# Attention's projection matmuls dealt 28 : 56 : 16 over a head pair's three steps

## The chip, the cores and the metric

The kernel runs on one core of a Trainium2 chip. The metric is the device time of one execution in microseconds, taken as the median of several runs. A core has five engines that work side by side and wait for each other through semaphores: TensorE (PE in the profile, with its weight loads as PEld), VectorE (DVE), ScalarE (ACT), GpSimd (POOL) and SyncE (SP), which here issues the DMAs.

## The reference

Two layers alternate, twice over, on a sequence of 2048 rows of width 640: an attention with a memory, and a gated mixer. Cut to what is computed:

```python
def attention(x, wq, wk, wv, wo, beta):          # 32 heads of 20, 4 segments of 512 rows
    for s in range(4):
        logits = q[s] @ k[s].T * scale + mask     # the mask adds -1e9 above the diagonal
        a_dot = softmax(logits) @ v[s]
        a_mem = (phi(q[s]) @ M) / (phi(q[s]) @ z + 1e-6)
        o[s] = g * a_mem + (1 - g) * a_dot        # g = sigmoid(beta), one per head
        M = M + phi(k[s]).T @ v[s];  z = z + sum(phi(k[s]))
    return o @ wo                                 # phi(t) = t + 1 where t > 0, else exp(t)

def mixer(x, w_in, w_sp, b_sp, w_out):
    z = gelu(x @ w_in);  z1, z2 = halves of z;  z2 = layernorm(z2)
    return (z1 * (w_sp @ z2 + b_sp)) @ w_out

x = x + attention(layernorm(x));  x = x + mixer(layernorm(x))   # and both once more
```

As its inputs say, q, k and v come from x through wq, wk and wv.

## The kernel before, in words

Each matrix is held as a pair of 16-bit parts, high and low, and a product is three matmuls: high by high, high by low, low by high. There are three stages per layer pair. `phase1a` (line 1082) is attention, `phase1b` (line 235) the last attention rows' output projection and the mixer's input projection, `phase2` (line 329) the mixer's spatial product and output projection. Attention alone is touched by the change; it runs twice.

Attention is written by hand as one order of work, in `Attention.run` (line 943). 128 rows of a segment and 128 rows of its keys meet in blocks; the blocks of one **head pair** (two heads, one segment) are dealt out over three **steps**. There are 64 head pairs, so 192 steps, and a few ahead and behind. At step t the loop at the end of `run` writes, in this order:

- `scores(n, c)` (line 829), c being t modulo 3. It makes two sets of score blocks in PSUM, each with a single buffer: `mp`, for the maxima of the pair two further on, which VectorE reduces to `mx` (line 871), and `es`, for the exponentials of this pair, which ScalarE writes to `P` (line 864). The rows of keys and queries are multiplied on line 855 and the mask is added by matmuls on line 827. In the first step the first block is 512 columns wide and there are 512 in all; in the second step the blocks are 384 and 128 wide, again 512; in the third, 256 only. The two heads of a pair go side by side. `mp` and `es` of a step can be written only when the reduction and the exponential of the step before have read them.
- what was posted for this step (`post`, line 548, puts a function on the list of a later step): evictions of the projections, key updates of the memory and others.
- `pvs` (line 896), the probability-times-value matmuls (line 908), for one head in the third step and for the other in the first. The second step has none. In the first step there is also `maxes` (line 885), which turns the maxima and stores them beside the queries by a DMA.
- `cast` (line 873), behind each `pvs`: ScalarE makes the 16-bit high part `PH` of a head's probabilities (line 881), GpSimd the low part `PL` (line 882). `combine` (line 912), VectorE's and GpSimd's work on a finished pair, comes in the second step, ahead of the scores.
- `until(t + 1)` (line 1043): all background streams that are due before the next step. There are four: the loads and layer norms (`fills`), weight preparation (`background`), the memory reads (`reads`, matmuls on lines 751 and 755), and **the projections** (`dense`, line 1003).

The projections are the q and k of a unit of heads (`unit`, line 678, matmuls on line 689, 512 columns wide), v of 128 rows (`value`, line 621, line 632, 320 wide) and the output projection of finished rows (`project`, line 650, line 665, 320 wide). All are groups of 15 matmuls into one of two PSUM buffers named `dn`. A group's eviction is posted one step after its end; for keys that feed the memory a second part (`keys`, line 720) is posted one step after that, and the buffer is read until its last operation on line 723. The stores of q and k (lines 798 and 799), the transposing DMA of the key features (line 725) and the loads of the pairs (`fetch`, line 803) are DMAs that SyncE issues in order.

When a projection matmul is due is a matter of a written table, not of measured times:

```python
PACE = (-LEAD, 2400), (0, 700), (53, 1150), (128, 1250), (END + G, 0)
```

It says from which step on how many nominal nanoseconds of projections go into a step. `step(w)` (line 964) turns the work done so far into a step with a fraction. `timed` (line 971) wraps each job: the job yields a nominal cost after each matmul (216 for q and k) or after three (408 for the narrow ones), and `timed` yields the time at which it wants to go on. So before the change the projections are spread evenly over the steps of a stretch of the table.

PE's instructions are issued in the order in which they are written (`manual_schedule` for PE, line 1085). The other engines' orders are a planner's, from the same program.

Of the kernel before, what the change touches and what calls it, by code (L numbers as in the profile page):

```python
# [454 lines left out]
KCH = ((0,), (1, 3), (2,))  # L455
QCH = ((3,), (2, 0), (1,))
BIG = 60000.0


def attn_consts(g, cp, beta):  # L460
# [6 lines left out]
    with tc.tile_pool(name="tmp", bufs=1) as tp, tc.tile_pool(name="acp", bufs=1, space=PSUM) as pp:  # L467
        f = tp.tile([128, 192], F32, name="fmask")
        for t, n, b, sg, op in ((g.big, 192, -64, 1, ALU.not_equal), (g.mask["q"], 128, 0, -1, ALU.is_ge), (g.mask["k"], 128, -64, 1, ALU.is_ge)):
            nc.vector.memset(f, 0.0)  # L470
            for h in range(2):
                v = f[64 * h:64 * h + 64, :n]
                nc.gpsimd.affine_select(v, v, [[sg, n]], op, BIG if op is ALU.not_equal else -BIG, base=b, channel_multiplier=-sg)
            nc.vector.tensor_copy(t, f[:, :n])
# [49 lines left out]
class Attention:  # L524
# [418 lines left out]
    def run(self, nseg=NSEG):  # L943
# [20 lines left out]
        def step(w):  # L964

            for (t, p), (e, _) in zip(PACE, PACE[1:]):
                if w <= p * (e - t):
                    return t + w / p
                w -= p * (e - t)

        def timed(it, done, work):
            end = done + work
            yield step(done)
            for w in it:
                done += w
                yield step(min(done, end))

        ev, jobs, acc = [], [], 0
        for c in order:
            w = V if c[0] in "vp" else U  # L980
            beg = step(acc)
            if c[0] in "vp":
                i = int(c[1:])
                s = i // 4
            if c[0] == "v":
                ev.append((beg - 11, 0, i))
                it = self.value(i)
                assert s < 2 or beg > G * (s - 1) + self.LV + 3, (i, beg)
            elif c[0] == "p":
                ev.append((beg - 3.5, 1, i))  # L990
                it = self.project(i)
                assert beg - 3.5 > G * (s + 1) + self.LV + 5, (i, beg)
            else:
                s, m = int(c[0]), int(c[1])
                it = self.unit(s, m)
                i = NU * s + m - 4
                for r in range(i, i + 1 + (i % NU < NU - 1)):
                    assert r < NU or beg > G * (r // NU) + 9 * (r % NU) - 3 + (3 if r % NU == 4 else 0), (s, m, r, beg)
                assert step(acc + w) < G * s + 9 * m - LEAD - 3, (s, m, step(acc + w))
            jobs.append(timed(it, acc, w))  # L1000
            acc += w
# [52 lines left out]
        for t in range(-LEAD, END):  # L1054
            self.now = t
            f, c = divmod(t + self.LF, 3)
            if c == 0 and 0 <= f + self.LM < N:
                self.fetch(f + self.LM)
            p, r = divmod(t - self.LV - 2, 3)
            if r == 0 and 0 <= p < N:  # L1060
                self.combine(p, *pairs[p])
            n, c = divmod(t, 3)
# [3 lines left out]
            for h in range(2):  # L1066
                p, r = divmod(t - self.LV - h, 3)
# [82 lines left out]
```

## Time and profile before

| what | value |
|---|---|
| median of 3 runs | 2474.31 us |
| lowest and highest | 2472.66, 2476.86 us |
| span of the profiled execution, first to last instruction | 2466.8 us |
| instructions | 50722 |
| mean granted TensorE clock | 0.974 of full speed |

The profiled execution's own time is known by its span alone: 2466.8 us, 7.5 us under the median of the runs, which holds also what lies before the first and after the last instruction. Attention lies at some 100 to 655 us of the span and at some 1300 to 1840 us.

In the profile's rows a group of instructions has its line, engine, operation, output and inputs by the program's names, shapes and count; behind the first bar the busy time and the mean length of one in ns, and behind the second the time for which the engine stood idle just before, with what ended it. In rows in order of time the first number is the start, the second the length, both in us from the span's start; brackets hold the idle time ahead. The durations of matmuls overlap, since they are pipelined; the distance from start to start is what one costs.

### The profile page before, as it was taken

What the parts mean: (1) busy time and instruction counts of PE and PEld (TensorE: products, weight loads), DVE (VectorE), ACT (ScalarE), POOL (GpSimd) and SP (SyncE); (2) the same over time, 40 slices, a digit from 0 to 9 for tenths busy, and PEclk for the clock granted to TensorE, in tenths of its full rate; (3) what the DMA queues carried; (4) which work ended last, traced back from release to release, by engine and by line L of the source; (5) the groups of instructions that cost most, each with busy time, mean ns of one, the idle gap of its engine ahead of it and who ended that gap; (6) DMA issues with size and microseconds to landing.
All of it is one profiled execution on the core that took longest, in us unless ns stands there. A gap on an engine that the chain in (4) does not pass through costs nothing.

```text
span 2466.8 us, 50722 instructions
## 1 busy us (share of the span) xinstructions
PE 2224.2 (90%) x20682; PEld 1317.4 (53%) x20682; DVE 1431.5 (58%) x2766; ACT 1137.3 (46%) x1388; POOL 937.1 (38%) x728
## 2 busy tenths in 40 slices
PE   3688888999899989999997888889997997999998
PEld 2355455666545545555554545565664554555554
DVE  8667877677754545544326777777764453453441
ACT  3278767777632222212124977777772222121110
POOL 3168777888610100000012988788872110000000
PEclk9899899999999999999999999999998998999999
DMA  6724644334553487767444352443446345766762
GB/s 198 207 56 101 172 107 113 100 108 123 140 162 94 114 221 193 189 155 173 101 137 124 74 123 69 112 113 86 126 128 145 94 114 151 167 166 155 173 128 58
DMA packets 502505, 325.00 MB, mean 132 GB/s; under 512 B 408512, under 2 KB 443456, under 8 KB 497152
## 3 DMA queue, kind: packets, MB, share of 16 engines
q1 hardware_dynamic: 502272, 321.76, 50.8%
q8 instruction: 162, 2.65, 0.5%
q14 instruction: 71, 0.58, 0.1%
HBM read 148.25 MB, written 85.34 MB: 95 GB/s over the span
## 4 chain that ended last, share of the span: by engine, by line
PE 56%; DVE 10%; ACT 10%; DMA 9%; issue 5%; SPq 3%; POOL 3%; ACTq 0%; DVEq 0%; POOLq 0%
PE gp L380 16%; PE zp L295 13%; PE cyp L409 6%; ACT PH L881 3%; ACT P L864 3%; PE vps L632 3%; PE pv L908 3%; DVE mx L871 3%; DMA wr<-in_B_w_sp_dram 2%; PE kps L689 2%; PE mp L855 2%; PE qps L689 2%; PE yps L665 2%; PE es L855 2%; POOL PL L882 2%
## 5 line engine op out<-in xcount | busy, mean ns | idle before, releaser
L882 POOL TENSOR_TENSOR PL<-P,PH 128x1280 f16<-128x1280 f32 x248 | 649.6, 2619 | 177.0 <-ACT PH L881 156.4
L380 PE MATMUL gp<-zh,wt 128*128 128x432 f16 x2048 | 466.6, 348 | 23.8 <-DMA wt<-wn 23.8
L871 DVE TENSOR_REDUCE mx<-mp 128x2 f32<-128x1024 f32 (+3 forms) x512 | 409.4, 816 | 130.2 <-PE mp L827 127.4
L380 PEld LDWEIGHTS <-wt 128*128 128x128 f16 x3072 | 301.8, 98 | 286.4 <-DMA wt<-wn 25.5
L864 ACT ACTIVATE P<-es,sc 128x1024 f32<-128x1024 f32 (+1 forms) x384 | 371.3, 967 | 161.6 <-PE es L827 160.0
L881 ACT CAST PH<-P 128x1280 f16<-128x1280 f32 x256 | 320.5, 1253 | 19.2 <-PE pv L908 12.8
L295 PEld LDWEIGHTS <-th 128*128 128x128 f16 x1920 | 188.6, 98 | 178.6 <-issue 10.4
L380 PE MATMUL gp<-zl,wt 128*128 128x432 f16 x1024 | 272.8, 348 | 0.0
L395 POOL MEMSET un<- 128x64 f16 x32 | 4.8, 151 | 672.5 <-DMA ut<-un 610.2
L205 POOL TENSOR_TENSOR lnrs<-lnve,mhalf 128x1 f32<-128x1 f32 x96 | 58.5, 617 | 467.7 <-DVE lnve L204 442.9
L855 PEld LDWEIGHTS <-qk 60*128 60x128 f16 (+1 forms) x2048 | 91.4, 93 | 261.3 <-issue 155.6
L383 ACT ACTIVATE u<-gp,bsp,un 128x864 f32<-128x864 f32 x32 | 34.2, 1070 | 363.3 <-PE gp L380 363.3
L357 DVE TENSOR_REDUCE am<-wr 128x1 f32<-128x2048 f32 x32 | 73.2, 2286 | 218.6 <-DMA wr<-in_B_w_sp_dram 218.6
L855 PE MATMUL mp<-qk 60*128 60x512 f16 (+3 forms) x1024 | 138.3, 307 | 55.9 <-DVE mx L871 55.0
L632 PE MATMUL vps<-wvh,xt 128*128 128x320 f16 x640 | 157.5, 310 | 27.2 <-DMA xt<-xnhl 14.5
L409 PE MATMUL cyp<-wuh,ut 128*128 128x320 f16 (+1 forms) x896 | 166.8, 303 | 11.9 <-DMA ut<-un 11.9
L855 PE MATMUL es<-qk 64*128 64x512 f16 (+3 forms) x1024 | 134.3, 298 | 47.3 <-ACT P L864 34.7
L409 PEld LDWEIGHTS <-ut 128*128 128x128 f16 (+1 forms) x1344 | 132.8, 99 | 69.9 <-DMA ut<-un 13.5
L827 PEld LDWEIGHTS <-big 64*128 64x128 f16 x3072 | 141.0, 95 | 50.5 <-issue 3.2
L908 PE MATMUL pv<-vs,PL 128*128 128x41 f16 x2560 | 163.0, 181 | 4.9 <-DVE PL L882 2.6
L908 PE MATMUL pv<-vs,PH 128*128 128x41 f16 x2560 | 166.3, 182 | 1.2 <-DVE ab L924 1.2
L295 PE MATMUL zp<-wi1h,th 128*128 128x432 f16 x640 | 150.2, 349 | 8.8 <-DMA th<-xnhl 8.8
(182 smaller groups left out, 4063.7 us busy)
## 6 DMA issues: line engine op xcount, KB each, us to landing
wr<-in_B_w_sp_dram SPq DMA_DIRECT2D x32, 1024.0 KB
qk<-st SPq DMA_DIRECT2D x256, 120.0 KB
x<-x SPq DMA_DIRECT2D x56, 320.0 KB
z<-z SPq DMA_DIRECT2D x32, 432.0 KB
cz<-z SPq DMA_DIRECT2D x32, 432.0 KB
xt<-in_A_x_dram SPq DMA_DIRECT2D x32, 320.0 KB
st<-qhl SPq DMA_DIRECT2D x40, 256.0 KB
st<-khl SPq DMA_DIRECT2D x40, 256.0 KB
```

Of the source, the lines that this page charges most:

```text
L295: nc.tensor.matmul(zp[:, n, :FHH], a[:, k, :], b[:, k, c:c + FHH], start=(k == 0 and j == 0), stop=(k == KD - 1 and j == 2))
L380: nc.tensor.matmul(gp[:, n, :FHH], wt[:, k // 8, a, k % 8, :], b[:, k, n * FHH:(n + 1) * FHH], start=(k == 0 and j == 0), stop=(k == NT - ...
L409: nc.tensor.matmul(yp[:, n, :320], a[:kn[k], k, :], b[:kn[k], k, n * 320:(n + 1) * 320], start=(k == 0 and j == 0), stop=(k == KO - 1 and ...
L632: nc.tensor.matmul(ps, a[:, k, c], b[:, k, n * 320:(n + 1) * 320], start=(i == 0), stop=(i == 14))
L689: nc.tensor.matmul(ps, a[:, k, c], b[:, k, :], start=(i == 0), stop=(i == 14))
L827: nc.tensor.matmul(out, g.big[r, 64 - 64 * s:192 - 64 * s], mk, start=False, stop=s == 1, skip_group_check=True)
L855: nc.tensor.matmul(out[:, h, o:o + w], a[r, ac], b[r, bc], start=o == 0, stop=False, skip_group_check=True)
L864: nc.scalar.activation(P[:, :, 512 * c:512 * c + ew], es[:, :, :ew], AF.Exp, scale=g.esc)
L871: nc.vector.tensor_reduce(self.mx[m][:, :, i], mp[:, :, o:o + w], AX.X, ALU.max)
L881: nc.scalar.copy(PH, P[:, h])
L882: (nc.gpsimd if h == 0 or n < self.N - self.TAIL else nc.vector).tensor_tensor(PL, P[:, h], PH, ALU.subtract)
L908: nc.tensor.matmul(pv[:, i, h, :], x[:, c:c + 128], v[:, j, h0 + h, :], start=(j == 0 and x is PH), stop=(j == i and x is PL), skip_group_ ...
```

## The change

A new constant gives three shares, and `share` maps a time within a head pair's three steps: the first 28 per cent of the pair's projection work goes behind the scores of its first step, the next 56 per cent behind the second, the last 16 behind the third. The amount per pair is the table's, as before. What is yielded inside a job goes through it; a job's first yield does not.

```diff
+DENSE = 0.28, 0.56, 0.16
...
+        def share(t):
+
+            p, r = divmod(t, 3)
+            done = 0
+            for c, f in enumerate(DENSE):
+                if r < 3 * (done + f) or c == 2:
+                    return 3 * p + c + min((r / 3 - done) / f, 0.999)
+                done += f
+
         def timed(it, done, work):
             end = done + work
             yield step(done)
             for w in it:
                 done += w
-                yield step(min(done, end))
+                yield share(step(min(done, end)))
```

## The prediction

> **What bounds the kernel now.** I read the page first, then the busy times by stretch, the groups with their forms kept apart, and the rows in order of time.
>
> ```profile
> span 2466.8 us, 50722 instructions
> ## 1 busy us (share of the span) xinstructions
> PE 2224.2 (90%) x20682; PEld 1317.4 (53%) x20682; DVE 1431.5 (58%) x2766; ACT 1137.3 (46%) x1388; POOL 937.1 (38%) x728
> ...
> PE 56%; DVE 10%; ACT 10%; DMA 9%; issue 5%; SPq 3%; POOL 3%; ACTq 0%; DVEq 0%; POOLq 0%
> ```
>
> Over the whole span PE is nearest to full, but only 56 per cent of the chain that ended last is PE; DVE and ACT hold 10 each. The change touches only the two attention stages, so I look at those, in three stretches that match the three paces of the projections: steps 12 to 59, 60 to 113, and 114 to 185.
>
> ```profile
> core 0: us, PE busy (x) PEld busy (x) DVE busy (x) ACT busy (x) POOL busy (x), PEclk, DMA share, GB/s
> 161.00:290.00 129.00, 108.17 (x1537) 63.58 (x1536) 101.74 (x196) 106.92 (x137) 105.03 (x64) 0.95 0.45 118
> 290.00:463.00 173.00, 150.68 (x1976) 94.36 (x1975) 130.93 (x252) 126.85 (x167) 131.01 (x93) 0.95 0.49 123
> 463.00:655.00 192.00, 183.97 (x2601) 119.44 (x2599) 139.78 (x276) 144.34 (x175) 156.43 (x106) 1.00 0.41 113
> ...
> 178.26:231.33 53.07, 47.74 (x737) 27.03 (x738) 41.92 (x81) 49.27 (x63) 48.01 (x28) 1.00 0.37 93
> ```
>
> In the first three rows the columns after the length are busy times. The third stretch is PE's: 184 of 192 us. In the second PE has 22 us of idle time, and no other engine is near full. The last row is an undisturbed part of the first stretch, 53.07 us long: ACT is busy for 49.27, POOL 48.01, PE 47.74. There ACT is the floor, and at most 53.07 - 49.27 = 3.8 us (7 per cent) can be had however PE's work is ordered.
>
> Where does PE wait? A step's chunk width tells it apart: 512 columns open the first step of a pair, 384 the second, 256 the third. So the idle time ahead of a form is the wait at the end of the step before.
>
> ```profile
> L855 PE MATMUL mp<-qk 60*128 60x512 f16 x256 | 51.3, 397 | 0.4 <-DVE mx L871 0.4
> L855 PE MATMUL es<-qk 64*128 64x512 f16 x256 | 49.4, 382 | 11.4 <-DMA qk<-mr 10.2 <-ACT P L864 0.9 <-ACT PH L881 0.3
> L855 PE MATMUL mp<-qk 60*128 60x384 f16 x256 | 43.4, 335 | 10.7 <-DVE mx L871 10.7
> L855 PE MATMUL es<-qk 64*128 64x384 f16 x256 | 41.9, 322 | 6.9 <-ACT P L864 6.3
> L855 PE MATMUL mp<-qk 60*128 60x256 f16 x256 | 36.3, 280 | 44.7 <-DVE mx L871 43.9
> L855 PE MATMUL es<-qk 64*128 64x256 f16 x256 | 35.7, 271 | 29.0 <-ACT P L864 27.5
> ```
>
> The idle time stands after the second bar. Ahead of the third step PE waits 44.7 + 29.0 = 73.7 us; ahead of the second 10.7 + 6.9 = 17.6; ahead of the first 0.4 and, for a DMA, 11.4. The wait sits behind the second step, the one step in which no probability-times-value matmuls run. One instance, in order of time:
>
> ```profile
> 201.75 0.39 PE L855 MATMUL mp<-qk 60*128 60x384 f16 x4
> 202.37 0.33 PE L827 MATMUL es<-maskk,big 64*128 64x128 f16 x4
> 202.85 0.59 PE L689 MATMUL qps<-xt,wqh 128*128 128x512 f16 x2
> 204.46 0.28 PE L855 MATMUL mp<-qk 60*128 60x256 f16 x2 [1.01 <-DVE mx L871]
> 205.78 0.38 PE L689 MATMUL qps<-xt,wql 128*128 128x512 f16 x1
> 206.00 0.59 PE L689 MATMUL qps<-xt,wqh 128*128 128x512 f16 x2
> 206.74 0.39 PE L855 MATMUL mp<-qk 60*128 60x512 f16 x2
> ...
> 202.71 0.50 DVE L924 TENSOR_TENSOR ab<-pv,rs 128x328 f32<-128x328 f32 x1
> 203.12 1.28 DVE L871 TENSOR_REDUCE mx<-mp 128x2 f32<-128x768 f32 x2
> 205.17 0.67 DVE L871 TENSOR_REDUCE mx<-mp 128x2 f32<-128x512 f32 x1
> ```
>
> The second step's scores and its three projections end by 203.44; VectorE reads the one score buffer until 204.40, after its combine work; the third step's scores start at 204.46. Behind the third step the maxima are ready at 205.84 and PE arrives at 206.74: a cushion of 0.90 us.
>
> **The change part by part.** It removes and adds no instruction; every matmul, load, eviction and DMA stays. Only the step behind which a projection matmul stands moves, inside its pair. Evaluating the code's own pace table gives the matmuls per step (first, second, third): first stretch 3.8, 3.4, 4.1 become 3.2, 6.0, 2.1; second 6.2, 6.2, 6.8 become 5.1, 10.9, 3.2; third 7.1, 7.5, 7.2 become 5.7, 12.5, 3.5. The granularity is fine enough for that: q and k matmuls move singly, the others in threes. From the rows above a q matmul takes 206.00 - 205.78 = 0.22 us of PE; one of the narrower kind takes 519.48 - 519.34 = 0.14:
>
> ```profile
> 519.34 0.30 PE L665 MATMUL yps<-woh,o 128*128 128x320 f16 x1
> 519.48 0.30 PE L665 MATMUL yps<-wol,o 128*128 128x320 f16 x1
> ```
>
> The first stretch is nearly all q and k, the second half and half, the third two thirds narrow. So the second step gains some 0.56, 0.85 and 0.8 us, the third loses 0.43, 0.65 and 0.6, the first 0.13, 0.19 and 0.22.
>
> *Waits ahead of the third step.* They fall by at most what the second step gains. The shares of the 73.7 us by stretch, first attention:
>
> ```profile
> L855 PE MATMUL mp<-qk 60*128 60x256 f16 x32 | 4.6, 287 | 9.2 <-DVE mx L871 9.2
> L855 PE MATMUL es<-qk 64*128 64x256 f16 x32 | 4.6, 276 | 4.6 <-ACT P L864 4.1
> ...
> L855 PE MATMUL mp<-qk 60*128 60x256 f16 x36 | 5.1, 280 | 7.7 <-DVE mx L871 7.7
> L855 PE MATMUL es<-qk 64*128 64x256 f16 x36 | 5.0, 271 | 6.2 <-ACT P L864 6.0
> ...
> L855 PE MATMUL mp<-qk 60*128 60x256 f16 x48 | 6.8, 279 | 4.8 <-DVE mx L871 4.5
> L855 PE MATMUL es<-qk 64*128 64x256 f16 x48 | 6.6, 269 | 2.6 <-ACT P L864 2.6
> ```
>
> That is 13.8, 13.9 and 7.4 us. Cutting each single wait at the gained time leaves some 7, 9.5 and 4.5 as coverable (a few waits are over 1.5 us and only partly covered); I take the second attention as like the first. What is realized of it I choose by the stretch's other engines. First stretch: ACT's 7 per cent room, so a third, 2 x 2.4 = 5 us. Second: idle PE, ACT and DVE at 73 to 76 per cent, so 60 per cent, 2 x 5.7 = 11. Third: PE-bound, a wait removed is time gained, 80 per cent, 2 x 3.6 = 7. Together 23 us; bounds 0 and 2 x 21 = 42. The steep start of each attention (steps before 12, no exponentials at first) I take as nothing, bounds 3 either way.
>
> *New waits ahead of the first and second steps.* The third step's cushion of 0.90 us covers 0.43 to 0.65; where it is smaller a little shows. The first step has less: PE already waits 17.6 us ahead of the second. If every one of the 128 pairs lost its first step's time anew, that is 128 x 0.2 = 26; at least nothing. Most pairs have no wait there, so I take 5 for both places.
>
> *The evictions behind the projections.* The accumulators have two buffers, and a group's eviction is written one step after its end (for keys a second part two steps after). A denser second step shortens the time until the buffer is wanted again. Such waits exist:
>
> ```profile
> PE kps L689 <- DVE phl L723: 25.6, 6, 8.3
> PE vps L632 <- DVE vs L638: 9.2, 4, 3.5
> ```
>
> By the code, groups reused under one step after their eviction is written rise from 5 to 8 in an attention. Three more in each of two attentions at 0.7 us are 4 us (25.6 / 6 and 9.2 / 4 are longer, but stand mostly at the start of an attention, where the paces crowd); bounds 0, and the 3.5 us of the longest value wait for all 16, 56.
>
> *DMAs and queues.* Each eviction takes its stores and its key transpose with it, on SP, earlier or later by under a step; they are read several steps on. The waits for a DMA (10.2 us ahead of the first step's scores) belong to the max rows, which keep their place, a whole pair ahead of use. I take nothing; a pair that gets shorter by 0.4 us takes as much cover from them, so up to 5 us. POOL gets no instruction moved, and its subtraction already ends late only where the cast before it does.
>
> Sum: -23 + 5 + 4 = -14 us. On the profiled span that is 2466.8 - 14 = 2452.8; the runs' median, 2474.3, lies 7.5 above the span, and I keep that distance: **2460 us**.
>
> The Trainium skill, Perfetto Trace Analysis, section Optimization Strategy, says that the same gap repeating on the engine that should be saturated can mean too little PSUM for the next tile. The trace agrees so far: the repeated wait is for the single score buffer, and no buffer is added here. By that rule alone the bubble would move instead of going, and the sum would be 0; it is the second rival.
>
> **The rivals.** *Evictions become the bound (slower).* Place: projection accumulators in the second and third stretch, where 11 to 12 projection matmuls, most of a group of 15, now run in one step. It decides once the key eviction's last VectorE operation ends after the third step's scores and its three matmuls. If the 16 close groups each stall PE by 2 us, between the 0.7 above and the 3.5, that is 32 in place of 4: -23 + 5 + 32 = +14, so 2488. Against it: PE waits for evictions little today outside the start. For it: DVE is 75 per cent busy and its queue is in order.
>
> *The bubble only moves (no change).* ACT's casts and exponentials hold 49.27 of 53.07 us in the clean part; if the second and third stretches follow ACT and DVE in the same way, the 23 shrinks to the 9 that new waits cost: 2474. For it: 27.5 us of the waits ahead of the third step end with ACT's exponential. Against it: ACT has 46 us of room in the second stretch's 173.
>
> *All is recovered (faster still).* 2 x 21 = 42 less 9 gives -33: 2441. It needs ACT to run full in the first stretch, which the 3.8 us there nearly forbid.
>
> That the change does not deal as it says I hold for excluded: PE's order is the written one.
>
> **How the numbers follow.** Forecast (2450 to 2468) 0.47, full recovery 0.13, no change 0.16, slower 0.24. A measurement of this kernel tells 0.2 per cent, 5 us, from no change. Faster takes the first two, 0.60; same 0.16; slower 0.24. The range reaches from full recovery, 2441, to the eviction rival, 2488, and leaves out about 0.07 below and 0.12 above. The forecast's own range is 2450 to 2468.
>
> **What would show it.** Right: idle time ahead of the 256-column forms falls from 73.7 to about 40 us, that ahead of the 384-column forms rises from 17.6 to some 20 to 25, and the third stretch's PE share rises. Wrong by evictions: waits of kps, qps, vps or yps for DVE grow by tens of us. Wrong by a moving bubble: the 384- and 512-column forms take over what the 256-column forms lose, with ACT's busy share unchanged. Wrong altogether would be a gain outside the two attention stages.

## The result and the profile after

The changed kernel takes 2444.64 us (median of 4 runs, 2440.32 to 2447.60) against 2473.48 (median of 4 runs of the kernel before beside them): a ratio of 0.9889, 95 per cent interval 0.9868 to 0.9910. That is 28.8 us off, about twice the 14 forecast. The spans of the two profiled executions differ by 28.2 us.

The page of the changed kernel, its span, its busy times and the engines' shares of the chain that ended last:

```profile
span 2438.6 us, 50718 instructions
## 1 busy us (share of the span) xinstructions
PE 2218.2 (91%) x20682; PEld 1319.0 (54%) x20682; DVE 1434.3 (59%) x2766; ACT 1133.7 (46%) x1388; POOL 936.1 (38%) x728
...
PE 60%; DVE 11%; DMA 11%; ACT 7%; issue 5%; POOL 3%; SPq 3%; ACTq 0%; DVEq 0%; POOLq 0%
```

PE's share of the chain rises from 56 to 60 per cent, ScalarE's falls from 10 to 7. The groups of the changed kernel with their forms apart show where PE now waits; idle time stands behind the second bar, and the lines shown carry a number one higher than before:

```profile
L856 PE MATMUL mp<-qk 60*128 60x512 f16 x256 | 50.8, 392 | 6.4 <-DVE mx L872 4.4 <-DVE lnve L204 0.8 <-DMA st<-khl 0.8
L856 PE MATMUL es<-qk 64*128 64x512 f16 x256 | 50.0, 384 | 15.1 <-DMA qk<-mr 12.3 <-ACT P L865 1.7 <-ACT PH L882 1.2
L856 PE MATMUL mp<-qk 60*128 60x384 f16 x256 | 43.3, 334 | 7.9 <-DVE mx L872 7.6
L856 PE MATMUL es<-qk 64*128 64x384 f16 x256 | 42.4, 325 | 9.6 <-ACT P L865 9.5
L856 PE MATMUL mp<-qk 60*128 60x256 f16 x256 | 36.3, 280 | 16.8 <-DVE mx L872 16.6
L856 PE MATMUL es<-qk 64*128 64x256 f16 x256 | 35.5, 271 | 16.8 <-ACT P L865 15.7
L890 PE MATMUL mtp<-ident,mx 128*8 128x128 f32 x128 | 34.9, 273 | 9.1 <-DVE gm L765 8.4 <-DVE mst L788 0.5
```

Ahead of the third step (256 columns) the wait falls from 73.7 to 16.8 + 16.8 = 33.6 us. Ahead of the second (384) it stays: 17.6 before, 17.5 now. Ahead of the first (512) it rises from 11.8 to 21.5. The last row is new as a wait: the transpose of the maxima, behind the first step's scores, had PE idle for 1.2 us ahead of it before and has 9.1 now. So 40.1 us went and 9.7 + 7.9 = 17.6 came.

One pair's second and third step of the changed kernel, in order of time (start, length; idle ahead in brackets). It is the pair that the prediction shows:

```profile
198.78 0.40 PE L856 MATMUL mp<-qk 60*128 60x384 f16 x4
199.00 0.34 PE L828 MATMUL mp<-maskq,big 64*128 64x256 f16 x4
199.19 0.40 PE L856 MATMUL es<-qk 64*128 64x384 f16 x4
199.40 0.34 PE L828 MATMUL es<-maskk,big 64*128 64x128 f16 x4
199.68 0.39 PE L690 MATMUL qps<-xt,wql 128*128 128x512 f16 x1
199.91 0.59 PE L690 MATMUL qps<-xt,wqh 128*128 128x512 f16 x2
200.34 0.38 PE L690 MATMUL qps<-xt,wql 128*128 128x512 f16 x1
200.55 0.38 PE L690 MATMUL qps<-xt,wqh 128*128 128x512 f16 x1
201.56 0.28 PE L856 MATMUL mp<-qk 60*128 60x256 f16 x2 [0.62 <-DVE mx L872]
```

Behind the second step's scores stand five q matmuls instead of three, and the third step's scores wait 0.62 us instead of 1.01. That is the change as meant: 0.4 us of work in a gap of one microsecond.

By stretch, from the changed kernel's busy times (length, PE, PEld, DVE, ACT, POOL with instruction counts; granted clock, DMA share, GB/s), and below them the same steps in the kernel before:

```profile
158.30:287.30 129.00, 107.35 (x1540) 62.89 (x1540) 104.07 (x197) 106.91 (x138) 104.58 (x64) 0.96 0.45 118
287.30:454.80 167.50, 146.76 (x1973) 94.03 (x1973) 132.78 (x251) 126.96 (x165) 131.02 (x93) 0.97 0.48 124
454.80:642.00 187.20, 182.91 (x2599) 119.63 (x2598) 137.98 (x277) 142.69 (x175) 155.90 (x106) 1.00 0.44 120
```

```profile
161.30:291.20 129.90, 109.07 (x1542) 63.95 (x1543) 102.94 (x198) 107.82 (x138) 104.73 (x64) 0.95 0.45 119
291.20:463.30 172.10, 149.78 (x1972) 94.02 (x1971) 129.73 (x250) 125.95 (x165) 131.01 (x93) 0.95 0.49 123
463.30:652.00 188.70, 181.31 (x2560) 117.72 (x2561) 136.78 (x273) 142.60 (x172) 154.77 (x105) 1.00 0.40 111
```

The first stretch hardly moves. The second loses 4.6 us. In the third PE goes from 181.31 of 188.70 us to 182.91 of 187.20, 96 to 98 per cent (this window takes in a little more work after the change). Measured from score start to score start, with the idle times of each stretch's groups added up, the two attentions together give (us, before to after; the last column is the difference):

| steps | wait ahead of the third step | of the second | at the first, with the transpose and the value matmuls | length |
|---|---|---|---|---|
| up to 11 | 4.5 to 1.4 | 4.7 to 5.2 | 0.0 to 0.0 | -4.1 |
| 12 to 59 | 27.3 to 15.1 | 4.6 to 8.9 | 2.6 to 11.1 | -4.4 |
| 60 to 113 | 27.5 to 14.6 | 8.4 to 3.1 | 3.8 to 12.4 | -13.6 |
| 114 to 179 | 9.0 to 0.0 | 0.0 to 0.0 | 1.9 to 3.1 | -8.3 |

The lengths sum to -30.4; the rest of the kernel gave back 2.3. The table holds the answer: everywhere the gap behind the second step about halves or goes. In the first stretch 12.2 us go and 12.8 come back at the other two steps; that it is shorter all the same goes with 2.3 us of waits for a key group's eviction, gone after the change, and with a PE that is busy for less time. In the second 8.6 come back at the first step, but 5.3 more go at the second; in the third almost nothing comes back.

### The profile page after: what moved, and what is told of

Its sections match the earlier page's. It is cut to its first block, busy times and chain, and to the rows that moved or that the text cites. A ratio compares the mean times of both kernels' runs of the same rounds, so it can differ in the third digit from the quotient of the medians.

```text
span 2438.6 us, 50718 instructions
## 1 busy us (share of the span) xinstructions
PE 2218.2 (91%) x20682; PEld 1319.0 (54%) x20682; DVE 1434.3 (59%) x2766; ACT 1133.7 (46%) x1388; POOL 936.1 (38%) x728
## 4 chain that ended last, share of the span: by engine, by line
PE 60%; DVE 11%; DMA 11%; ACT 7%; issue 5%; POOL 3%; SPq 3%; ACTq 0%; DVEq 0%; POOLq 0%
PE gp L380 16%; PE zp L295 14%; PE cyp L409 6%; PE pv L909 3%; PE yps L666 3%; PE kps L690 3%; DMA wr<-in_B_w_sp_dram 3%; PE vps L633 3%; PE mp L856 3%; PE qps L690 3%; ACT PH L882 2%; ACT P L865 2%; PE es L856 2%; POOL PL L883 2%; DVE mx L872 2%
## 5 line engine op out<-in xcount | busy, mean ns | idle before, releaser
L295 PEld LDWEIGHTS <-th 128*128 128x128 f16 x1920 | 188.9, 99 | 177.8 <-issue 11.7
L383 ACT ACTIVATE u<-gp,bsp,un 128x864 f32<-128x864 f32 x32 | 34.2, 1068 | 355.5 <-PE gp L380 355.5
L633 PE MATMUL vps<-wvh,xt 128*128 128x320 f16 x640 | 156.3, 310 | 22.5 <-DMA xt<-xnhl 13.8
L409 PEld LDWEIGHTS <-ut 128*128 128x128 f16 (+1 forms) x1344 | 132.6, 99 | 73.7 <-DMA ut<-un 17.4
L367 ACT ACTIVATE wn<-wr,ivw 128x1024 f16<-128x1024 f32 x64 | 71.9, 1144 | 194.6 <-DVE ivw L362 111.1
```

What stands on the lines that cost most here:

```text
L295: nc.tensor.matmul(zp[:, n, :FHH], a[:, k, :], b[:, k, c:c + FHH], start=(k == 0 and j == 0), stop=(k == KD - 1 and j == 2))
L409: nc.tensor.matmul(yp[:, n, :320], a[:kn[k], k, :], b[:kn[k], k, n * 320:(n + 1) * 320], start=(k == 0 and j == 0), stop=(k == KO - 1 and ...
L633: nc.tensor.matmul(ps, a[:, k, c], b[:, k, n * 320:(n + 1) * 320], start=(i == 0), stop=(i == 14))
```

## The experiments

The theory at this point: the gain is projection work laid into the gap behind the second step, less new waits where the work was taken away. Rivals: the gain comes from elsewhere (the start, the order of evictions, the granted clock), or VectorE and ScalarE set the pace and the bubble only moves. Each ratio is to the kernel before on the same chip, with its 95 per cent interval.

**How far to deal.** Half the change:

```diff
-DENSE = 0.28, 0.56, 0.16
+DENSE = 0.31, 0.44, 0.25
```

> Deal 31:44:25, half way between the even deal and the changed one. Theory A (each matmul moved behind the second step covers its own PE time of the wait there, whatever ScalarE and VectorE do): the first half of the cover is worth more than the second, since some waits are shorter than the cover; idle time ahead of the 256-column forms falls from 73.7 to 48-52 us (the changed kernel has 33.6), ratio to before about 0.993, some 2455 us. Theory B (what is covered is bounded by ScalarE and VectorE, so the gain comes from the light third step and jumps): ratio 0.997 or more, or as low as the full change, 0.989.

Measured: 2452.03 us, 0.9911 (0.9896 to 0.9926), a larger gain than theory A had with more wait left than it had. Ahead of the third step PE waits 38.5 + 21.6 = 60.1 us, the first part in this row:

```profile
L856 PE MATMUL mp<-qk 60*128 60x256 f16 x256 | 36.5, 282 | 38.5 <-DVE mx L872 23.4 <-DVE lnve L204 14.6
```

The third stretches are as short as with the whole change (169.9 and 171.6 us from 174.1 and 176.1); the second ones hardly gain (171.0 and 164.8 from 172.2 and 164.0), and the row shows a wait there that the kernel before has not, 14.6 us for a layer norm's work on VectorE (`lnve`). One more wait is longer in this kernel: the value projections (`vps`) wait 9.8 us for the keys' evictions, 3.5 in the kernel before.

The same and more of it, `DENSE = 0.24, 0.64, 0.12`:

> Deal 24:64:12, further the same way. Theory A with a floor: 33.6 us are left ahead of the 256-column forms, in few long waits that 0.2 us more covers little: 27-30 us left; new waits ahead of the 512- and 384-column forms grow by as much or more; ratio 0.987 to 0.992, level with the changed kernel. The eviction rival: bursts of 7 to 14 matmuls in the second step meet accumulators not yet read, waits of kps, qps, vps and yps for VectorE grow by over 10 us, ratio 0.994 or more.

Measured: 2439.29 us, 0.9855 (0.9834 to 0.9875). Waits ahead of the third step 18.9 + 11.8 = 30.7. The waits for evictions, in the waits of PE of this kernel (total, times, longest):

```profile
PE kps L690 <- DVE phl L724: 24.4, 4, 9.8
PE vps L633 <- DVE vs L639: 9.9, 8, 3.1
```

They were 25.6 and 9.2 before. Even a denser second step doesn't make evictions the bound. The ratio is a little under what either expectation had.

The deal turned round, `DENSE = 0.28, 0.16, 0.56`, so that the second step has the least:

> Deal 28:16:56, the second and third share exchanged: the second step, the one that waits, loses half of its projections. Theory A: each of 128 pairs loses 0.36 to 0.55 us of cover, so idle time ahead of the 256-column forms rises from 73.7 to 115-135 us; the other forms lose under 10; ratio 1.015 to 1.022, 2510 to 2528 us. Theory B (the waits follow ScalarE and VectorE, and a heavy third step gives them the time): ratio 1.000 to 1.006.

Measured: 2559.36 us, 1.0344 (1.0328 to 1.0359), dearer than either theory had it. The waits are as the theory wants them, 86.8 + 45.8 = 132.6 us:

```profile
L856 PE MATMUL mp<-qk 60*128 60x256 f16 x256 | 37.0, 286 | 86.8 <-DVE mx L872 77.3 <-DVE lnve L204 8.4
L856 PE MATMUL es<-qk 64*128 64x256 f16 x256 | 37.1, 280 | 45.8 <-ACT P L865 44.3
```

That is 59 us more, and 13 more ahead of the second step, less 10 ahead of the first. Of the 87 us by which the span grew, 33 are PE's own: it is busy for 2257.3 us instead of 2224.2 with as many instructions, at a mean granted clock of 0.960 instead of 0.974. More of that in the last section.

**Which step should give the work.** The second step gets its half from the third alone; the first keeps its third:

```diff
-DENSE = 0.28, 0.56, 0.16
+DENSE = 0.3334, 0.5, 0.1666
```

> Deal 33:50:17, the first step keeps its third, only the third step gives. Theory A: idle time ahead of the 256-column forms about 40 us, and the new idle time ahead of the 512-column forms (0.4 + 11.4 before, 6.4 + 15.1 after) stays as in the changed kernel, since that is behind the third step; ahead of the 384-column forms under the 17.5 of both. Ratio 0.990 to 0.992, within 5 us of the changed kernel. Theory B: the lighter first step is what lets the exponentials of the first step start early; without it half of the gain goes, ratio 0.995.

Measured: 2436.30 us, 0.9843 (0.9828 to 0.9858), the shortest of all kernels that do the whole computation, and ahead of the kernel before and the changed one. Its groups:

```profile
L856 PE MATMUL mp<-qk 60*128 60x512 f16 x256 | 50.9, 393 | 5.9 <-DVE mx L872 5.6
L856 PE MATMUL es<-qk 64*128 64x512 f16 x256 | 49.7, 382 | 8.5 <-DMA qk<-mr 5.1 <-ACT PH L882 2.0 <-ACT P L865 1.2
...
L856 PE MATMUL mp<-qk 60*128 60x256 f16 x256 | 36.7, 283 | 29.1 <-DVE mx L872 25.6 <-DVE lnve L204 2.9
L856 PE MATMUL es<-qk 64*128 64x256 f16 x256 | 35.9, 274 | 17.2 <-ACT P L865 16.1
...
L890 PE MATMUL mtp<-ident,mx 128*8 128x128 f32 x128 | 34.8, 272 | 3.7 <-DVE rs L920 2.6 <-DVE mst L788 1.1
```

Ahead of the third step it waits 12.7 us more than the changed kernel does (46.3), ahead of the first 7.1 less (14.4), at the transpose 5.4 less (3.7), ahead of the second 4.2 less (7.5 + 5.8). So against this deal the changed kernel loses more at the steps it took from than it covers at the third. Both theories fail here: each had less of a gain, and theory A had the wait ahead of the first step as long as in the changed kernel.

More still for the first step, at the second's cost, `DENSE = 0.40, 0.44, 0.16`:

> Deal 40:44:16: the third step as light as in the changed kernel, the first heavier than even. If the new waits ahead of the second step and of the maxima's transpose come from the lighter first step, they fall below those of before (under 12 us ahead of the 384-column forms); the second step covers less, some 50-55 us ahead of the 256-column forms. Ratio 0.985 to 0.989.

Measured: 2436.64 us, 0.9866 (0.9836 to 0.9895); waits ahead of the third step 27.1 + 16.6 = 43.7, fewer than expected. But the new waits don't go with the heavier first step: 15.0 us ahead of the second, where under 12 was expected, 20.9 ahead of the first and 5.5 at the transpose, against 11.8 and 1.2 with even shares. A light first step is thus not their only cause. And taking from the third alone, but more, `DENSE = 0.33, 0.57, 0.10`:

> Deal 33:57:10: the second step as heavy as in the changed kernel, what the first step keeps is taken from the third. Ahead of the 256-column forms as in the changed kernel, 30-36 us; ahead of the 512-column forms and DMA waits 18-25 us, since the third step has under 2 matmuls in the first stretch; ratio 0.983 to 0.987, level with 33:50:17.

Measured: 2449.33 us, 0.9914 (0.9893 to 0.9936). Waits ahead of the third step 27.5 + 11.7 = 39.2, ahead of the first 10.2 + 13.7 = 23.9; the third stretches are back at 174.4 and 174.8 us, as long as before the change. The expectation, level with 33:50:17, failed: 9.5 us more wait ahead of the first step than there, and 4.3 more at the transpose. With a tenth the third step covers less of the first step's buffers.

All deals side by side, idle time of PE in us by where it stands, from the groups of each kernel:

| shares | third step | second | first | transpose | sum | ratio |
|---|---|---|---|---|---|---|
| 28 : 16 : 56 | 132.6 | 30.7 | 1.4 | 0.4 | 165.1 | 1.0344 |
| even | 73.7 | 17.6 | 11.8 | 1.2 | 104.3 | 1 |
| 33 : 57 : 10 | 39.2 | 18.6 | 23.9 | 8.0 | 89.7 | 0.9914 |
| 31 : 44 : 25 | 60.1 | 10.4 | 12.6 | 3.1 | 86.2 | 0.9911 |
| 40 : 44 : 16 | 43.7 | 15.0 | 20.9 | 5.5 | 85.1 | 0.9866 |
| 24 : 64 : 12 | 30.7 | 25.8 | 19.9 | 5.6 | 82.0 | 0.9855 |
| 28 : 56 : 16 (the change) | 33.6 | 17.5 | 21.5 | 9.1 | 81.7 | 0.9889 |
| 33 : 50 : 17 | 46.3 | 13.3 | 14.4 | 3.7 | 77.7 | 0.9843 |

The time goes roughly with the sum of the four columns and not with the third step's wait alone. From half the change on, the third step's wait halves again while the sum stays between 78 and 90. The columns leave out PE's waits for the evictions of the projections (kps, vps, qps and yps for VectorE's reads of them), and these differ too: 40.2 us with even shares, 46.0 with 31:44:25, 36.3 with the change, 35.2 with 24:64:12. The 10.8 us between 31:44:25 and 24:64:12 are most of the 12.7 by which their times differ, where the columns differ by 4. The optimum is broad: of the best four only 33:50:17 and the change have intervals that don't touch.

**Where in attention.** The deal in steps 60 to 113 alone:

```diff
-                yield share(step(min(done, end)))
+                u = step(min(done, end))
+                yield share(u) if 60 <= u < 114 else u
```

> The deal 28:56:16 in the second stretch alone (steps 60 to 113), even elsewhere. Theory A (each stretch pays by itself): the second stretches fall from 172 and 164 us to 167 and 155, the first and third stay within 2 us of before, ratio 0.993 to 0.996. Theory B (the stretches are coupled, or the split seen in the trace is chance): the second stretches stay over 170 and 162, ratio 0.998.

Measured: 2448.55 us, 0.9920 (0.9896 to 0.9944); its second stretches take 168.1 and 157.2 us from 172.2 and 164.0. That is 10.9 us; the profiled span is 18.3 us under that of the kernel before, and the other 7.4 lie in parts that this edit doesn't touch, so they are not shown to be the deal's. The same with `-99 <= u < 12`, the start alone:

> The deal in the start of each attention alone (steps before 12), even elsewhere. The prediction had nothing here. Theory A from the trace: the starts shrink from 60.4 and 61.0 us to 57.5 and 59.8, 4 us in all, ratio 0.997 to 0.9985, with the accumulator waits there as before. If the start's gain in the changed kernel came from later stretches: no change.

Measured: 2465.68 us, 0.9981 (0.9963 to 1.0000). The starts take 59.8 and 58.9 us, 0.6 and 2.1 less. Stretches that this edit doesn't touch differ by up to 5 us from those of before (168.7 against 164.0), so single stretches of single profiles are good to a few us only. In the table by steps the second stretch is the largest part of the change's gain; whether the start gains is not settled.

**Is ScalarE the floor of the first stretch?** The cast and GpSimd's subtraction do 640 of 1280 columns, and the value matmuls read those twice. This leaves out half of the probabilities' split; first with even shares, then with the change:

```diff
-        nc.scalar.copy(PH, P[:, h])
+        nc.scalar.copy(PH[:, :640], P[:, h, :640])
...
-                c = POFF[j] + 128 * (i - j)
+                c = (POFF[j] + 128 * (i - j)) % 640
```

> The kernel before, even deal, with half of the probabilities' split left out: ScalarE casts and GpSimd subtracts 640 of 1280 columns, the value matmuls read those twice, so PE's work stays. ScalarE loses some 1.2 us a pair, GpSimd 2.5. If the wait ahead of the third step is made by VectorE and by the step's own length, the first stretch shrinks little under the even deal: from 130 to 122-127 us, and 10 us or more of idle time stay ahead of the third step there.

> The changed kernel with the same half split left out. If ScalarE (93 per cent busy in the clean part) is what kept the first stretch at 129 us under the new deal, it now falls to 116-120 us, more than the even deal gains by the same cut; if ScalarE is not the floor there, it stays within 3 us of the even one with the cut.

Measured: 2441.81 us, 0.9896 (0.9874 to 0.9918), and 2423.52 us, 0.9818 (0.9793 to 0.9842). The first stretches, even shares on top, the change below, in each the first attention and then the second (columns as above):

```profile
157.50:283.20 125.70, 104.85 (x1542) 62.47 (x1543) 98.81 (x196) 91.32 (x137) 65.46 (x64) 0.96 0.45 121
1346.60:1469.00 122.40, 103.51 (x1537) 61.38 (x1536) 92.48 (x181) 86.67 (x130) 65.43 (x64) 0.96 0.42 104
```

```profile
154.00:277.70 123.70, 107.58 (x1540) 64.41 (x1540) 99.62 (x198) 92.09 (x138) 66.26 (x64) 0.93 0.46 122
1344.30:1459.40 115.10, 102.03 (x1537) 60.62 (x1537) 91.96 (x181) 86.88 (x130) 65.36 (x63) 0.99 0.46 110
```

ScalarE drops from 108 to 92 us and GpSimd from 105 to 66, yet with even shares the first attention's stretch is only 4.2 us shorter and the second's not at all (122.4, before 121.5): PE still waits 15.0 + 4.7 us ahead of its third steps, for VectorE first. So ScalarE isn't the floor under the even deal, as that expectation had it.

Under the change the stretch of the first attention is 2.0 us under the even one, within the 3 that were to mean that ScalarE isn't the floor there either; that of the second attention is 7.3 us under. Together 9.3 us, in place of the 4.4 of the table above: more, but by no more than single stretches of single profiles can be off. In the whole kernel the deal is worth less with the split halved: 18.3 us (2441.81 to 2423.52) in place of 28.8, and the four columns fall by 13.9 us (87.8 to 73.9) in place of 22.6. Whether ScalarE and GpSimd hold the deal back in the first stretch stays open.

**Who holds the single buffers?** The maxima are taken over the first half of each block's columns, which leaves out the other half; again with even shares and with the change:

```diff
-                nc.vector.tensor_reduce(self.mx[m][:, :, i], mp[:, :, o:o + w], AX.X, ALU.max)
+                nc.vector.tensor_reduce(self.mx[m][:, :, i], mp[:, :, o:o + w // 2], AX.X, ALU.max)
```

> Even deal; each maximum is taken over the first half of its columns only, which leaves out half of VectorE's reductions (1.22 to some 0.65 us, 0.95 + 0.41 to some 0.85) and nothing of PE or ScalarE. If the wait ahead of the third step is the length of what follows the scores on VectorE: its part, 43.9 us, falls under 15, ScalarE's exponential takes part of it over (27.5 to 30-40), ratio 0.985 to 0.992. If not, VectorE's part stays over 30 and the ratio over 0.995.

> The changed kernel with the same half of the reductions left out. If the deal gains by covering the wait behind the second step, it gains less where less wait is left: its ratio to red_even is 0.992 to 0.996 in place of 0.989. If the deal gains by something else, the same 0.989 against red_even.

Measured: 2444.77 us, 0.9901 (0.9878 to 0.9924), and 2417.74 us, 0.9781 (0.9767 to 0.9796). The waits ahead of the third step, even shares first, then the change:

```profile
L855 PE MATMUL mp<-qk 60*128 60x256 f16 x256 | 36.3, 280 | 20.6 <-DVE mx L871 20.2
L855 PE MATMUL es<-qk 64*128 64x256 f16 x256 | 36.2, 273 | 46.1 <-ACT P L864 45.8
```

```profile
L856 PE MATMUL mp<-qk 60*128 60x256 f16 x256 | 36.2, 280 | 11.2 <-DVE mx L872 8.3 <-DVE lnve L204 2.9
L856 PE MATMUL es<-qk 64*128 64x256 f16 x256 | 35.4, 270 | 23.0 <-ACT P L865 22.6
```

With shorter reductions the wait doesn't go: 24 us less behind VectorE, 17 more behind ScalarE's exponential, 66.7 in all. (VectorE's part stays over the 15 expected, ScalarE's goes over its 30 to 40.) The kernel is nevertheless 27.7 us shorter, and the four columns of the table above account for only half of that (104.3 to 90.8), so the ratio, which was forecast rightly, comes for the most part not from the wait ahead of the third step. The deal covers that wait as well, 66.7 to 34.2, and its gain is the whole one: 0.9781 / 0.9901 = 0.988, against 0.9889 alone. The expectation that the deal would be worth less here fell with the reason for it.

**Is it the order of VectorE's work?** In the pair shown in the prediction VectorE does its combine work ahead of the second step's reduction. Three edits tried to put it behind: the combine written behind the scores (with even shares and with the change), and one step later.

```diff
+            n, c = divmod(t, 3)
+            self.scores(n, c)
             p, r = divmod(t - self.LV - 2, 3)
             if r == 0 and 0 <= p < N:
                 self.combine(p, *pairs[p])
-            n, c = divmod(t, 3)
-            self.scores(n, c)
```

> The kernel before with the even deal; the finished pair's combine (0.16 + 0.20 + 0.50 us of VectorE) is written behind the second step's scores in place of ahead of them. If the wait ahead of the third step is made by VectorE's order (theory A's cause: the reduction starts behind the combine), VectorE's share of it, 43.9 us, falls to 15-25 us with no projection moved, ratio 0.991 to 0.995. If the planner starts the combine first anyway, or ScalarE's exponential then ends last, under 0.2 per cent changes.

> The changed kernel with the combine behind the second step's scores. 16.6 us of waits for VectorE are left ahead of the 256-column forms: with VectorE's order as the cause they fall to some 8 us, ratio 0.985; if it is not the cause, as the changed kernel, 0.989.

```diff
-            p, r = divmod(t - self.LV - 2, 3)
+            p, r = divmod(t - self.LV - 3, 3)
```

> Even deal, the combine of a finished pair written one whole step later, ahead of the third step's scores, so that it can't stand before the second step's reduction. If VectorE's order there is what PE waits for: VectorE's part of the idle time ahead of the 256-column forms falls from 43.9 to 15-25 us; the value matmuls of the third step, which need the combine's buffer, wait up to 5-15 us; ratio 0.990 to 0.996. If the reductions' own length is the cause: within 0.2 per cent.

> The deal 33:50:17 with the combine one step later. With VectorE's order as the cause, the 25.6 us of waits for it ahead of the 256-column forms fall to 10-15 us, ratio 0.979 to 0.983 against 0.9843 without. If not, or if the value matmuls wait instead, 0.984 to 0.988.

Measured: 2471.75 us, 0.9993 (0.9982 to 1.0004), and 2445.44 us, 0.9884 (0.9869 to 0.9899); one step later 2469.17 us, 1.0007 (0.9993 to 1.0021) with even shares, and 2441.16 us, 0.9879 (0.9858 to 0.9901) with the shares of the best version. In every one the trace still has the combine ahead of the reduction in over nine of ten pairs, as before. One instance of the kernel with even shares and the combine one step later, VectorE's rows in order of time:

```profile
202.98 0.50 DVE L924 TENSOR_TENSOR ab<-pv,rs 128x328 f32<-128x328 f32 x1
203.39 1.28 DVE L871 TENSOR_REDUCE mx<-mp 128x2 f32<-128x768 f32 x2
```

VectorE's order is the planner's, and it kept it. So these runs say nothing on the question; whether the combine's place makes the wait stays open. The last one bears on another: the same shares 33:50:17 read 0.9843 without the edit and 0.9879 with it, though the four columns sum to 77.7 and 75.6 us. So the lead of 33:50:17 over the change is no firmer than that.

**Can the new waits be had cheaper?** In the changed kernel the maxima's transpose waits 9.1 us. It is moved behind the projections of its step; `both` does this and the combine edit:

```diff
-                if h == 1 and c == 0 and 0 <= n - 1 + self.LM < N:
-                    self.maxes(n - 1 + self.LM)
...
             until(t + 1)
+            if c == 0 and 0 <= n - 1 + self.LM < N:
+                self.maxes(n - 1 + self.LM)
```

> The changed kernel with the transpose of the maxima written behind the first step's projections in place of ahead of them. The changed kernel has 8.4 us of the transpose waiting for VectorE's read of the memory product (gm), in a buffer that both use. If that is a cost of the light third step, it goes, and the max rows land 0.3 to 1 us later: waits for their DMA, 12.3 us, grow by 0 to 10. Ratio 0.986 to 0.990.

> The changed kernel with both: combine behind the scores, maxima behind the projections. If both are causes and independent, ratio 0.982 to 0.986; if neither, 0.989.

Measured: 2446.76 us, 0.9889 (0.9873 to 0.9905), and 2451.66 us, 0.9907 (0.9890 to 0.9923). The transpose's wait falls from 9.1 to 1.0 us, but the scores of the first step wait 24.3 us instead of 21.5 (14.8 of it for the max rows' DMA instead of 12.3), and the third step's 40.0 instead of 33.6. 8.1 us were covered and 10.0 came back, 0.8 of them ahead of the second step. In `both` the transpose waits 0.9 us and the third step's scores 41.1; neither cause brought its gain.

## Why the prediction came out half right

The direction, the place and the mechanism were right: the wait behind the second step was covered by the work laid there, and new waits came where work was taken. What failed are sizes in the sum -23 + 5 + 4. First of all the step "What is realized of it I choose by the stretch's other engines ... Together 23 us": 40.1 us went. The two costs behind it failed as well: 17.6 us of new waits for the 5, and none for the 4 of evictions.

- **Waits ahead of the third step.** 42 us were worked out as coverable and 23 taken. 40.1 went (73.7 to 33.6). The sign that the prediction gave, "to about 40 us", doesn't fit its own sum, which leaves 73.7 - 23 = 50.7. By stretch 12.2, 12.9 and 9.0 us went, of 14, 19 and 9 coverable, where 5, 11 and 7 were taken. The discount for busy engines was far too large in the first stretch, where a third was taken and nearly all went; there the price came as new waits at the other steps, and not as a smaller cut. Another 6.0 went in the start and behind step 179.
- **New waits.** 5 us taken, bounds 0 and 26; 17.6 measured, all at the first step: 9.7 ahead of its scores and 7.9 at the transpose, which the prediction had not on its list. Ahead of the second step, where 20 to 25 was forecast, the sum is unchanged (17.5), made of +4.3 in the first stretch and -5.3 in the second; why it fell there no run tells.
- **What was counted twice.** 40.1 less 17.6 is 22.5, close to the discounted 23. In the second and third stretch the cut less the new waits is 9.6 and 7.8 us, against the 11 and 7 taken. There the discount alone came out at about the price of the new waits, and 5 us for them were charged on top. In the first it is -0.6 against the 5 taken. That the sum fits all the same is luck: the start and the end of the attentions make up the 5.7 that are missing.
- **Evictions.** 4 us taken, 32 in the rival. kps waits 25.6 us for VectorE before and after, vps 8.6 instead of 9.2, and all four waits of projections for evictions fall from 40.2 to 36.3. The denser deal (`more`) did not raise them; only the half deal did, to 46.0. The rival was mis-sized by all of its price: the denser second step costs nothing at the two buffers here.
- **The start.** 0 taken, bounds 3 either way; 4.1 us shorter in the profile, not settled by the run of the start alone.
- **The bubble only moves.** This rival held for the first stretch, where 12.8 us came back for the 12.2 that went; whether ScalarE and GpSimd are behind that, the cast runs leave open. It failed in the other two.
- **The rest.** 28.2 less 22.5 leaves 5.7 us, for which the prediction had no term. Waits for evictions are 3.9 us less, other waits 4.2 us more (3.5 of them in the mixer, for a DMA), and PE's busy time is 6.0 less (2224.2 to 2218.2). But kernels with even shares show PE busy for 2224.2 to 2235.6 us at spans within 0.3 us of each other, so why those 6.0 went stays open.
- **The base.** The profiled execution's distance of 7.5 us from the median was no constant: the change's profiled execution took 2440.32 us as a run, and its span is 2438.6, 1.7 less. If it was the same before the change, the larger part of the 7.5 was one run's distance from the others. It cost the forecast nothing as a difference.

The time also came out near the rival "all is recovered" (2441). Its cut came nearly, 40.1 of 42 us, but not its costs: the new waits are over three times the 5 that it charged, and what made up for them, evictions and PE's busy time, it had not. That the two times lie 4 us apart is luck.

The Trainium skill, Perfetto Trace Analysis, section Optimization Strategy, says that such a repeated gap can mean too little PSUM. The trace agrees that the single score buffer is what PE waits for. The prediction's second rival took from it that without a buffer the bubble stays; it did not, 73.7 us became 33.6 with none added.

## What to carry to other kernels

Work that nothing waits for soon is worth most in the gap behind a step whose buffer is read late; deal it by the measured gap of each step, and count the waits of all steps, since those it is taken from pay (here 17.6 us of the 40.1). If a saving is discounted for engines that may become late, do not charge the new waits again. When one reader of a pair of buffers is made faster, look at the other before expecting the wait to go.

## What the runs showed of the hardware

With longer waits the granted clock was lower. In the turned-round deal the first stretch reads (columns as above):

```profile
159.30:310.00 150.70, 116.44 (x1542) 68.15 (x1543) 105.29 (x199) 109.80 (x139) 107.06 (x64) 0.89 0.42 106
```

The same 1542 matmuls that held PE for 109.07 us at a granted clock of 0.95 hold it for 116.44 at 0.89, and the stretch has 34.3 us of idle time instead of 20.8. Over the whole kernel its four runs had clocks of 0.958 to 0.961, those of the kernel before beside them of 0.970 to 0.974. So the 87 us are more than the added waits. That the waits lowered the clock is not shown, and idle time alone doesn't set it: with the split halved, the change's first stretch idles for 16.1 us at 0.93 (123.70 less 107.58), the even one for 20.9 at 0.96.

The Trainium skill, TensorE: Matmul & The Clock Gate, section "Why this matters for your kernels", advises against PE idle gaps over some 3 us between bursts. In the turned-round stretch the longest of 17 waits for `mp` is 3.8 us and the longest of 6 for `es` 3.7. But the same stretch of the kernel before has no wait over 2.2 us and a clock of 0.95. So gaps of that length are not the only ones that go with a lower clock here; whether the few long waits or the many short ones matter, no run tells apart.
